# Preparing the first two pairs of a clustered attention: cluster choice on PSUM operands for pair 0, through GpSimd for pair 1, and another order of squares, halves and copies

## The chip, the cores and the metric

The kernel runs on one core of a Trainium2 chip. The metric is the device time of one execution in microseconds; lower is better. The core's engines are named as the profile names them: PE (TensorE matmuls) and PEld (its weight loads), DVE (VectorE), ACT (ScalarE), POOL (GpSimd) and SP (SyncE, whose queue issues all DMAs of this kernel). Each engine executes its own instructions in the order in which they are written for it and meets the others only at semaphores.

## The reference

Attention over clusters, for 2 batches of 8 heads, 768 positions, head width 64 and 16 centroids per head, and then two two-layer networks (512 to 2048 to 512) over its 1536 rows:

```python
q_n = q / (np.linalg.norm(q, axis=-1, keepdims=True) + 1e-06)      # k_n, c_n alike
q_assign = np.argmax(np.einsum('bhsd,hcd->bhsc', q_n, c_n), axis=-1)
k_assign = np.argmax(np.einsum('bhsd,hcd->bhsc', k_n, c_n), axis=-1)
mask = q_assign[:, :, :, None] == k_assign[:, :, None, :]
scores = scale * np.matmul(q, k.transpose(0, 1, 3, 2))
scores = np.where(mask, scores, -1000000000.0)
attn = softmax(scores)                                             # rows without the maximum
x = np.matmul(attn, v)
h = x @ w_in;  x = (np.maximum(h, 0.0) + alpha * np.minimum(h, 0.0)) @ w_out
h = x @ w_in2; out = (np.maximum(h, 0.0) + np.log1p(np.exp(-np.abs(h)))) @ w_out2
```

## The kernel before, in words

**Pairs and units.** Heads go in pairs: 8 pairs, numbered 0 to 7. A pair has 12 units: 2 heads by 6 blocks of 128 queries. Unit u computes the scores of 128 queries against 768 keys (lines 571 and 572), their row maxima (`nm`, line 577, on DVE), the exponentials (`e`, line 586, on ACT), transposes of these on PE (`pt`, line 599), their high half on ACT (`ph`, line 615) and the remainder on DVE (`pl`, line 619), and the product with the values (`o`, line 629). The stages of a unit are spread over the turns of one loop: in turn u PE does the scores of unit u, the transposes of unit u-2 and the product of unit u-4; DVE does the maximum of unit u and the remainders of unit u-2. After some 240 us the two networks follow, which the change leaves alone. All products of 32-bit numbers are made from a high half and a low half of each operand (`hi` and `lo`).

**Preparation of a pair.** Before its units a pair n needs:

- `sq0`, `sq1`: squares of its q and k by token (tile `sq` from `tok`), in two halves, on ACT for pairs 0 and 1 and on POOL for later ones; the second half also issues the load of the next pair's `tok`.
- Sums of the squares: for pair 0 by `red0` and `red1` on DVE, for later pairs by `fold0` to `fold2` on POOL, six additions of halves in place (line 341).
- `inv`: one over the norm, in three steps by `inv_norm` (lines 127 to 136): a logarithm and an exponential on ACT; a reciprocal on DVE and a product and a sum on the engine `eng` (lines 132 and 133); a scaling (line 135) and a reciprocal on DVE.
- `hik`, `lok`, `hiq`, `lq0`, `lq1`: high and low halves of k and q by dimension (from `dim`); `op0`, `op1`: six DMAs for each head that copy them into the operands `ak`, `aq`, `mk`, `mq` (line 521).
- `dk`, `dq` (or `dh`, `dl`), `de`, `dt`: dot products with the centroids (`dps`), and their transposition by token (`dt`, in PSUM).
- The cluster choice by token: `dn` scales the dots by the norms (line 428), `mx` finds the largest of 16 (line 440), `eq` compares with it and multiplies by a rank (lines 448 and 449), `m2` finds the largest rank (line 459), subtracts it (line 462) and clips at -1 (line 463). The result `oh` is 0 at the chosen cluster and -1 elsewhere.
- `ot0`, `ot1`: `oh` transposed on PE; `mr`, `rq`, `rk`: mask rows made of it by one multiplication and one addition with `mscale` and `mbias`, into `mrow` or straight into `mq` and `mk`. `va`: the halves of v, a cast on DVE and a subtraction on POOL, which then issues the load of the next pair's v.

**What sets the order.** The preparation of pair 0 and the beginning of pair 1 are written out in the list `PRELUDE`; "warm n" puts n idle transposes on PE. Everything else has a due turn in the tables `FIRST` (pair 0), `SECOND` (pair 1), `THIRD` (pair 2) and `STEADY`: an entry x of pair n is placed in turn 12(n-2) + x, rounded up, at the end of the turn if x is a whole number and ahead of its transposes otherwise. PE, ACT and DVE keep the order in which the code is written; for POOL and SP a scheduler puts the instructions in order. So what DVE does in turn 0 to 4 of pair 0 is mixed with the preparation of pair 1, whose entries lie at 12 to 16.

Of the kernel before, what the change touches and what calls it, by code (L numbers as in the profile page):

```python
# [9 lines left out]
F32 = mybir.dt.float32  # L10
# [3 lines left out]
AF = mybir.ActivationFunctionType  # L14
ALU = mybir.AluOpType
# [9 lines left out]
    hik=-1, lok=3, sq0=0, hiq=2, sq1=2, fold0=3, fold1=4, fold2=6, lq0=5, dk0=4, dq0=6, de0=6.5,  # L25
    inv0=7, lq1=8, inv1=9, dk1=9, dq1=10, inv2=10, de1=10.5, dt=11, dn=11, op0=11, mx=11.5, eq=15,
    m2=16, va=18, ot0=19, mr0=19, op1=19, ot1=20.5, mr1=20.5, mk0=20.5, mk1=20.5, go=22,
)
FIRST = dict(
    mr0=23.5, mr1=23.5, mk1=23.5,  # L30
)
SECOND = dict(
    dl0=12, dl1=12, inv0=12, de0=12.5, de1=12.5, inv1=13, inv2=13, dt=13, dn=14, mx=14, op0=14,
    eq=15, m2=16, va=18, ot0=19, mr0=19, op1=19, ot1=20.5, mr1=20.5, mk0=20.5, mk1=20.5, go=22,
)
THIRD = dict(
    hik=3, lok=3, sq0=0, hiq=4, sq1=2, fold0=4, fold1=5, fold2=6, lq0=5, dk0=5, dq0=6, de0=6.5,
    inv0=7, lq1=8, inv1=9, dk1=9, dq1=10, inv2=10, de1=10.5, dt=11, dn=11, op0=11, mx=11.5, eq=15,
    m2=16, va=18, ot0=19, mr0=19, op1=19, ot1=20.5, mr1=20.5, mk0=20.5, mk1=20.5, go=22,
)  # L40
PRELUDE = [
# [6 lines left out]
]  # L48

FINISH = [7, 9, 10, 12, 12, 14, 16]  # L50
# [3 lines left out]
P = 128  # L54
BIG = float(2.0**100)
# [3 lines left out]
def kernel(  # L59
# [20 lines left out]
    nc = tc.nc  # L80
    B, NPAIR, _, _, S = qk_dim.shape
    H = 2 * NPAIR
    C = P // H
    D = P // 2
# [10 lines left out]
    HC = 2 * C  # L95
    SCALE = float(D) ** -0.5

    const = ctx.enter_context(tc.tile_pool(name="const", bufs=1))
# [15 lines left out]
    mscale = const.tile([2 * HC, 1], F32, name="mscale")  # L114
    nc.gpsimd.memset(mscale, 1.0)
    nc.gpsimd.memset(mscale[HC : 2 * HC], BIG)
    mbias = const.tile([2 * HC, 1], F32, name="mbias")
    nc.gpsimd.memset(mbias, 1.0)
    nc.gpsimd.memset(mbias[HC : 2 * HC], 0.0)
    alpha_sb = const.tile([P, NF], F32, name="alpha_sb")  # L120
    nalpha = const.tile([P, NF], F32, name="nalpha")

    def inv_norm(out_, ss, pool, tag, eng):

        n = ss.shape[1]
        s0 = pool.tile([P, n], F32, tag=tag + "a", name="s0")
        nc.scalar.activation(out=s0, in_=ss, func=AF.Ln, bias=tiny)
        nc.scalar.activation(out=s0, in_=s0, func=AF.Exp, scale=0.5)
        yield
        s1 = pool.tile([P, n], F32, tag=tag + "b", name="s1")  # L130
        nc.vector.reciprocal(out=s1, in_=s0)
        eng.tensor_tensor(out=s1, in0=ss, in1=s1, op=ALU.mult)
        eng.tensor_tensor(out=s1, in0=s1, in1=s0, op=ALU.add)
        yield
        nc.vector.tensor_scalar(out=s1, in0=s1, scalar1=0.5, scalar2=1e-6, op0=ALU.mult, op1=ALU.add)
        nc.vector.reciprocal(out=out_, in_=s1)
        yield
# [53 lines left out]
    with ExitStack() as actx:  # L191
        ap3 = actx.enter_context(tc.tile_pool(name="ap3", bufs=3))
        first_ctx = ExitStack()
        ap1 = first_ctx.enter_context(tc.tile_pool(name="ap1", bufs=1, side="right"))
        ap2 = actx.enter_context(tc.tile_pool(name="ap2", bufs=2))
        ap4 = actx.enter_context(tc.tile_pool(name="ap4", bufs=1))
        ps_s = actx.enter_context(tc.tile_pool(name="ps_s", bufs=2, space=PSUM))
# [13 lines left out]
        ops = {}  # L211
# [80 lines left out]
        n_ = J * 4  # L292
        every = [P, n_, C]
# [3 lines left out]
        def steps_of(n):  # L297
# [49 lines left out]
            def inv():  # L347
                if "gen" not in q:
                    ss = q["ss"] if first_ else q["sq"][:, :, 0:1].rearrange("p n o -> p (n o)")
                    q["gen"] = inv_norm(q["rinv"], ss, ap1, "n", nc.vector if early else nc.gpsimd)  # L350
                next(q["gen"])

            for k in range(3):
# [70 lines left out]

            @step("dn")
            def _():
                q["dn"] = ap1.tile(every, F32, tag="dn", name="dn")
                nc.vector.tensor_tensor(
                    out=q["dn"],
                    in0=q["dt"][:, 0 : n_ * C].rearrange("p (n c) -> p n c", c=C),  # L430
                    in1=q["rinv"][:, :, None].to_broadcast(every),
                    op=ALU.mult,
                )


            @step("mx")
            def _():
                dn = q["dn"]
                q["mx"] = ap1.tile([P, n_], F32, tag="mx", name="mx")
                nc.vector.tensor_reduce(out=q["mx"], in_=dn, axis=AX.X, op=ALU.max)  # L440
                if not early:
                    nc.gpsimd.tensor_tensor(out=dn, in0=dn, in1=q["mx"][:, :, None].to_broadcast(every), op=ALU.subtract)

            @step("eq")
            def _():
                dn, r_ = q["dn"], rank[:, None, :].to_broadcast(every)
                if early:
                    nc.vector.tensor_tensor(out=dn, in0=dn, in1=q["mx"][:, :, None].to_broadcast(every), op=ALU.is_equal)  # L448
                    nc.vector.tensor_tensor(out=dn, in0=dn, in1=r_, op=ALU.mult)
                else:  # L450
                    nc.vector.scalar_tensor_tensor(
                        out=dn, in0=dn, scalar=0.0, in1=r_, op0=ALU.is_equal, op1=ALU.mult
                    )

            @step("m2")
            def _():
                dn = q["dn"]
                m2 = ap1.tile([P, n_], F32, tag="m2", name="m2")
                nc.vector.tensor_reduce(out=m2, in_=dn, axis=AX.X, op=ALU.max)
                q["oh"] = ap1.tile([P, J, 4 * C], F32R, tag="oh", name="oh")  # L460
                eng = nc.vector if first_ else nc.gpsimd
                eng.tensor_tensor(out=dn, in0=dn, in1=m2[:, :, None].to_broadcast(every), op=ALU.subtract)
                eng.tensor_scalar(
                    out=q["oh"], in0=dn.rearrange("p (j n) c -> p j (n c)", j=J), scalar1=-1.0, scalar2=None, op0=ALU.max
                )

            def onehot(t):
# [4 lines left out]
                for j in range(3):  # L472
                    nc.tensor.transpose(q["ot", t][0 : 2 * HC, j * P : (j + 1) * P], q["oh"][:, 3 * t + j, :], identr)

            def rows(t, eng):
                if t == 0:
                    q["mrow"] = ap1.tile([2 * HC, 2, HS], F32R, tag="mrow", name="mrow")
                src = q["ot", t].bitcast(F32)[0 : 2 * HC, 0:HS]
                if eng is nc.scalar:
                    nc.scalar.activation(out=q["mrow"][:, t, :], in_=src, func=AF.Identity, scale=mscale, bias=mbias)  # L480
                else:
                    nc.vector.tensor_scalar(
                        out=q["mrow"][:, t, :], in0=src, scalar1=mscale, scalar2=mbias, op0=ALU.mult, op1=ALU.add
                    )

            def straight(t, s_):

                _, _, mq, mk = res[0]
                src = q["ot", t].bitcast(F32)[:, 0:HS]
                if s_ == 0:  # L490
                    nc.scalar.activation(
                        out=mq[D : D + C, halves[t]], in_=src[0:C], func=AF.Identity, scale=mscale[0:C], bias=mbias[0:C]
                    )
                else:
                    nc.vector.tensor_scalar(
                        out=mk[D : D + C, halves[t]], in0=src[HC : HC + C], scalar1=mscale[HC : HC + C],
                        scalar2=mbias[HC : HC + C], op0=ALU.mult, op1=ALU.add,
                    )

            for t in range(2):  # L500
# [47 lines left out]
            @step("go")  # L548
            def _():
                for hh in range(2):  # L550
                    ops[n, hh] = (*res[hh], q["vv"])

            return st_

# [67 lines left out]

        def attend(key, part):
            n, hh, g = key
            vv = ops[n, hh][4]
            if part == 0:
                acc[key] = ps_o.tile([P, 512], F32, tag="o", name="o")
            for j in range(J):
                nc.tensor.matmul(  # L629
                    acc[key][:, 0:QG],  # L630
                    lhsT=vv[:, j, 2 * hh : 2 * hh + 2, :].rearrange("p a d -> p (a d)"),
                    rhs=grp[key][part][:, j, :],
                    start=part == 0 and j == 0,
                    stop=part == 1 and j == J - 1,
                )
# [386 lines left out]
```

## Time and profile before

| | us |
|---|---|
| Time, median of 3 runs (lowest, highest) | 824.72 (823.08, 827.33) |
| Time of the profiled execution | 823.56 |
| Its span, first to last instruction | 821.8 |
| PE busy | 793.8 |
| DVE busy | 603.1 |
| ACT busy | 490.7 |
| POOL busy | 345.1 |

The time is that of the whole execution, the span that of its instructions; 1.76 us of the profiled execution lie around the span. The page has the busy time of each engine, the span in 40 slices, and the chain of work that ended last, followed back from the end. What the change touches lies in the first 45 us, so the timeline of single engines in that stretch says more than the sums.

### The profile page before, as it was taken

The page shows a single profiled execution, that of the slowest core. Times are in us where ns is not written, and L with a number is a line of the kernel's source. Part 1 is how long each engine was busy: PE and PEld are TensorE (multiplying, and loading weights), DVE is VectorE, ACT ScalarE, POOL GpSimd, SP SyncE. Part 2 cuts the span into 40 slices and gives each one's busy share as a digit, 9 for nine tenths or more (in the row PEclk, how much of TensorE's full clock was granted, in tenths as well). Part 3 has the DMA queues.
Part 4 walks back from the last instruction along what each step waited for, and adds up shares of the span by engine and source line. Part 5 has one row for each costly group of instructions (what it writes and reads, how often), then busy time and mean ns, then how long its engine had stood idle before and what let it go on. Part 6 is the DMA issues. An engine that isn't in the chain of part 4 may idle for free.

```text
span 821.8 us, 11917 instructions
## 1 busy us (share of the span) xinstructions
PE 793.8 (97%) x4124; PEld 667.6 (81%) x4124; DVE 603.1 (73%) x957; ACT 490.7 (60%) x992; POOL 345.1 (42%) x350
## 2 busy tenths in 40 slices
PE   6799999999998879999999999999999999999997
PEld 5699998999997758888888888888888888888885
DVE  7899999999999977348547636977468469655443
ACT  4689998999898687247346435664355245243221
POOL 6566866775434664027025214574153045023000
PEclk9699999999999989999999999999999999999999
DMA  9876685665532254012202301411023013000102
GB/s 274 228 175 161 164 204 133 156 158 117 115 100 84 78 179 134 21 51 78 77 26 77 103 1 51 154 52 51 1 76 130 1 52 102 1 1 1 51 27 76
DMA packets 27195, 76.50 MB, mean 93 GB/s; under 512 B 4512, under 2 KB 7456, under 8 KB 27136
## 3 DMA queue, kind: packets, MB, share of 16 engines
q1 hardware_dynamic: 27136, 75.75, 32.2%
q8 instruction: 32, 0.52, 0.3%
q14 instruction: 27, 0.22, 0.1%
HBM read 49.36 MB, written 3.15 MB: 64 GB/s over the span
## 4 chain that ended last, share of the span: by engine, by line
PE 87%; DVE 7%; ACT 2%; DMA 1%; issue 1%; POOL 1%; DVEq 0%; SPq 0%; ACTq 0%; POOLq 0%
PE acc L887 33%; PE hp L828 31%; PE o L629 7%; PE pt L599 7%; PE s L572 4%; PE s L571 4%; PE dps L393 2%; DVE pl L619 1%; DVE nm L577 1%; DVE r L169 1%; DMA mk<-mrow 1%; POOL t L174 1%; DMA tok<-in_qk_tok_dram 1%; DVE m L167 0%; DVE dn L448 0%
## 5 line engine op out<-in xcount | busy, mean ns | idle before, releaser
L828 PE MATMUL hp<-xh,ih 128*128 128x512 f32 x384 | 152.3, 398 | 2.2 <-DVE gl L869 2.2
L828 PE MATMUL hp<-xl,ih 128*128 128x512 f32 x384 | 152.4, 397 | 0.0
L828 PE MATMUL hp<-xh,il 128*128 128x512 f32 x384 | 152.2, 397 | 0.0
L177 POOL TENSOR_TENSOR il<-t,ih 128x512 fp32r<-128x512 f32 x32 | 44.0, 1375 | 206.7 <-ACT ih L176 197.8
L869 DVE TENSOR_TENSOR gl<-hp,gh 128x512 fp32r<-128x512 f32 x96 | 65.9, 687 | 75.8 <-ACT gh L868 75.7
L868 ACT CAST gh<-hp 128x512 fp32r<-128x512 f32 x96 | 56.3, 586 | 93.3 <-PE acc L887 81.8
L619 DVE TENSOR_TENSOR pl<-pt,ph 128x384 fp32r<-128x384 f32 x192 | 97.4, 547 | 1.7 <-ACT ph L615 1.1
L174 POOL TENSOR_TENSOR t<-m,r 128x512 uint32<-128x512 uint32 x64 | 85.3, 1333 | 29.3 <-DVE r L169 16.4
L577 DVE TENSOR_REDUCE nm<-s 128x1 f32<-128x768 f32 x96 | 91.0, 948 | 7.8 <-PE s L572 7.4
L586 ACT ACTIVATE e<-s,nm 128x768 f32<-128x768 f32 x96 | 87.9, 916 | 7.3 <-DVE nm L577 7.0
L599 PE MATMUL pt<-ident,e 128*128 128x128 f32 x576 | 83.6, 279 | 5.8 <-DVE pl L619 5.7
L828 PEld LDWEIGHTS hp<-xh,ih 128*128 128x128 f32 x384 | 72.3, 188 | 20.1 <-DVE gl L869 2.7
L615 ACT CAST ph<-pt 128x384 fp32r<-128x384 f32 x192 | 83.5, 490 | 8.4 <-PE pt L599 7.4
L850 ACT ACTIVATE sp<-a 128x512 f32<-128x512 f32 x48 | 30.4, 633 | 96.2 <-DVE a L846 96.2
L828 PEld LDWEIGHTS hp<-xh,il 128*128 128x128 f32 x384 | 72.4, 189 | 17.6
L828 PEld LDWEIGHTS hp<-xl,ih 128*128 128x128 f32 x384 | 72.4, 189 | 17.2
L599 PEld LDWEIGHTS pt<-ident,e 128*128 128x128 f32 x576 | 67.7, 142 | 15.3 <-DVE pl L619 11.0
L887 PE MATMUL acc<-gh,oh 128*128 128x512 f32 x192 | 75.0, 402 | 4.3 <-ACT gh L868 4.3
L887 PE MATMUL acc<-gl,oh 128*128 128x512 f32 x192 | 77.0, 401 | 0.0
L887 PE MATMUL acc<-gh,ol 128*128 128x512 f32 x192 | 76.5, 399 | 0.0
L887 PE MATMUL acc<-ol,gh 128*128 128x512 f32 x192 | 75.9, 395 | 0.0
L887 PE MATMUL acc<-oh,gh 128*128 128x512 f32 x192 | 75.7, 395 | 0.0
(168 smaller groups left out, 1671.3 us busy)
## 6 DMA issues: line engine op xcount, KB each, us to landing
raw<-in_w_in_dram SPq DMA_DIRECT2D x32, 512.0 KB, 3.3
raw<-in_w_out_dram SPq DMA_DIRECT2D x32, 512.0 KB, 3.3
tok<-in_qk_tok_dram SPq DMA_DIRECT2D x8, 768.0 KB, 5.2
ak<-hi SPq DMA_DIRECT2D x32, 192.0 KB, 3.2
dim<-in_qk_dim_dram SPq DMA_DIRECT2D x6, 768.0 KB, 5.9
rawv<-in_v_dram SPq DMA_DIRECT2D x8, 384.0 KB, 3.2
aq<-hi SPq DMA_DIRECT2D x16, 192.0 KB, 3.7
mq<-hi SPq DMA_DIRECT2D x16, 192.0 KB, 4.0
```

Source lines behind the costliest of these rows:

```text
L174: nc.gpsimd.tensor_tensor(out=t.bitcast(U32), in0=mu, in1=r, op=ALU.add)
L177: nc.gpsimd.tensor_tensor(out=low, in0=t, in1=high.bitcast(F32), op=ALU.subtract)
L577: nc.vector.tensor_reduce(out=nm, in_=st[u]["s"][:, :, 0:HS], axis=AX.XY, op=ALU.max, negate=True)
L586: nc.scalar.activation(out=e.rearrange("p (a j) c -> p a (j c)", a=2), in_=st[u]["s"][:, :, 0:HS], func=AF.Exp, bias=st[u]["nm"], scale=1. ...
L599: nc.tensor.transpose(pt[:, j * P : (j + 1) * P], st[u]["e"][:, 3 * a + j, :], ident)
L615: nc.scalar.copy(out=dh, in_=src)
L619: nc.vector.tensor_tensor(out=dl, in0=src, in1=dh.bitcast(F32), op=ALU.subtract)
L629: nc.tensor.matmul(acc[key][:, 0:QG], lhsT=vv[:, j, 2 * hh : 2 * hh + 2, :].rearrange("p a d -> p (a d)"), rhs=grp[key][part][:, j, :], st ...
L828: nc.tensor.matmul(hp, lhsT=a_[:, cs], rhs=b_[:, c, ts], start=n == 0, stop=n == 3 * NC_ - 1)
L868: nc.scalar.copy(out=gh, in_=hp)
L869: nc.vector.tensor_tensor(out=gl, in0=hp, in1=gh.bitcast(F32), op=ALU.subtract)
L887: nc.tensor.matmul(accs[c], lhsT=a_, rhs=b_, start=opens and n == 0, stop=closes and n == 2)
```

## The change

For pair 0: the tile `dn` of the cluster choice lies in a slot of the PSUM pool `ps_s` and not in SBUF; `m2` makes `oh` by one comparison (1 at the chosen cluster, 0 elsewhere) and not by a subtraction and a clip; a second bias `mbias0` (0 and -2^100) fits the mask rows to that. `va` moves from `PRELUDE` to the end of turn 0. In `PRELUDE` the high half of k (`hik 0`) comes ahead of the second half of the squares (`sq1 0`), `rk0` ahead of `rk1`, and the second "warm" has 18 transposes, not 5.

For pair 1: the choice takes the form of the later pairs, a subtraction on POOL behind `mx` and one instruction on DVE for `eq` (due at 15.5, not 15), and the product and the sum of `inv` go to POOL. `go` hands over the pair's dictionary and not the tile `vv`, since `vv` is made later.

```diff
 FIRST = dict(
-    mr0=23.5, mr1=23.5, mk1=23.5,
+    mr0=23.5, mr1=23.5, mk1=23.5, va=24,
 )
 SECOND = dict(
...
-    eq=15, m2=16, va=18, ot0=19, mr0=19, op1=19, ot1=20.5, mr1=20.5, mk0=20.5, mk1=20.5, go=22,
+    eq=15.5, m2=16, va=18, ot0=19, mr0=19, op1=19, ot1=20.5, mr1=20.5, mk0=20.5, mk1=20.5, go=22,
...
-    "warm 5", "sq0 0", "centroids_high", "red0 0", "centroids_low", "sq1 0", "red1 0", "hik 0",
+    "warm 18", "sq0 0", "centroids_high", "red0 0", "centroids_low", "hik 0", "sq1 0", "lok 0",
...
+    mbias0 = const.tile([2 * HC, 1], F32, name="mbias0")
+    nc.gpsimd.memset(mbias0, 0.0)
+    nc.gpsimd.memset(mbias0[HC : 2 * HC], -BIG)
...
-                    q["gen"] = inv_norm(q["rinv"], ss, ap1, "n", nc.vector if early else nc.gpsimd)
+                    q["gen"] = inv_norm(q["rinv"], ss, ap1, "n", nc.vector if first_ else nc.gpsimd)
...
             @step("dn")
             def _():
-                q["dn"] = ap1.tile(every, F32, tag="dn", name="dn")
+                if first_:
+                    s_ = ps_s.tile([P, 2, 512], F32, tag="s", name="dn")
+                    q["dn"] = s_[:, 0, 0 : n_ * C].rearrange("p (n c) -> p n c", c=C)
+                else:
+                    q["dn"] = ap1.tile(every, F32, tag="dn", name="dn")
...
-                if not early:
+                if not first_:
                     nc.gpsimd.tensor_tensor(out=dn, in0=dn, in1=q["mx"][:, :, None].to_broadcast(every), op=ALU.subtract)
 
             @step("eq")
             def _():
                 dn, r_ = q["dn"], rank[:, None, :].to_broadcast(every)
-                if early:
+                if first_:
...
-                eng = nc.vector if first_ else nc.gpsimd
-                eng.tensor_tensor(out=dn, in0=dn, in1=m2[:, :, None].to_broadcast(every), op=ALU.subtract)
-                eng.tensor_scalar(
+                if first_:
+                    nc.vector.tensor_tensor(
+                        out=q["oh"].rearrange("p j (n c) -> p (j n) c", c=C), in0=dn,
+                        in1=m2[:, :, None].to_broadcast(every), op=ALU.is_equal,
+                    )
+                    return
+                nc.gpsimd.tensor_tensor(out=dn, in0=dn, in1=m2[:, :, None].to_broadcast(every), op=ALU.subtract)
+                nc.gpsimd.tensor_scalar(
...
+            bias = mbias0 if first_ else mbias
...
-                    ops[n, hh] = (*res[hh], q["vv"])
+                    ops[n, hh] = (*res[hh], q)
```

DVE in turns 1 to 4, before: behind the maxima of units 0 and 1 comes the whole middle part of pair 1's `inv` (tile `s_378`, `rinv`), ahead of the maximum of unit 2.

```order
L577 TENSOR_REDUCE nm<-s 128x1 x2
L131 RECIPROCAL s_378<-s_359 128x24
L132 TENSOR_TENSOR s_378<-sq,s_378 128x24
L133 TENSOR_TENSOR s_378<-s_378,s_359 128x24
L135 TENSOR_SCALAR s_378<-s_378 128x24
L136 RECIPROCAL rinv<-s_378 128x24
L577 TENSOR_REDUCE nm<-s 128x1
L619 TENSOR_TENSOR pl<-pt,ph 128x3x128 x2
```

So DVE makes product and sum (lines 132 and 133) itself. The same place of DVE now (line numbers are larger by 4 to 15):

```order
L592 TENSOR_REDUCE nm<-s 128x1
L556 CAST vv<-rawv 128x6x64 x2
L592 TENSOR_REDUCE nm<-s 128x1
L135 RECIPROCAL s_393<-s_374 128x24
L139 TENSOR_SCALAR s_393<-s_393 128x24
L140 RECIPROCAL rinv<-s_393 128x24
L592 TENSOR_REDUCE nm<-s 128x1
L634 TENSOR_TENSOR pl<-pt,ph 128x3x128 x2
```

The casts of v stand between the first two maxima, and between the reciprocal and the scaling of `s_393` DVE now waits for two instructions of POOL.

POOL at that place, before: the subtractions for `vv` stand ahead of pair 1's folds, and behind the folds come the squares of pair 2 (`sq<-tok`).

```order
L542 TENSOR_TENSOR vv<-rawv,vv 128x6x64 x2
L367 TENSOR_TENSOR lo<-dim,hi 128x768
L341 TENSOR_TENSOR sq<-sq 128x24x32
L341 TENSOR_TENSOR sq<-sq 128x24x16
L341 TENSOR_TENSOR sq<-sq 128x24x8
L341 TENSOR_TENSOR sq<-sq 128x24x4
L341 TENSOR_TENSOR sq<-sq 128x24x2
L341 TENSOR_TENSOR sq<-sq 128x24
L322 TENSOR_TENSOR sq<-tok 128x768 x2
L341 TENSOR_TENSOR sq<-sq 128x24x32
```

There is nothing for pair 1's `inv` on POOL. POOL now, from the end of pair 1's folds:

```order
L345 TENSOR_TENSOR sq<-sq 128x24
L557 TENSOR_TENSOR vv<-rawv,vv 128x6x64 x2
L136 TENSOR_TENSOR s_393<-sq,s_393 128x24
L326 TENSOR_TENSOR sq<-tok 128x768
L137 TENSOR_TENSOR s_393<-s_393,s_374 128x24
L326 TENSOR_TENSOR sq<-tok 128x768
L345 TENSOR_TENSOR sq<-sq 128x24x32
L345 TENSOR_TENSOR sq<-sq 128x24x16
L450 TENSOR_TENSOR dn<-dn,mx 128x384
L345 TENSOR_TENSOR sq<-sq 128x24x8
L371 TENSOR_TENSOR lo<-dim,hi 128x768
```

The subtractions for `vv` have moved behind the folds, and the two instructions on `s_393` that DVE waits for stand on either side of the first half of pair 2's squares.

SP's queue, before, from the load of pair 1's `tok` through the copies of pair 0's operands to the load of v for pair 1:

```order
L234 DMA tok<-in_qk_tok_dram 128x1536
L521 DMA ak<-hi 64x768 x2
L521 DMA aq<-hi 64x768
L521 DMA mq<-hi 64x768
L521 DMA mk<-lo 64x768
L521 DMA aq<-lo 64x768
L521 DMA ak<-hi 64x768 x2
L521 DMA mk<-lo 64x768
L239 DMA rawv<-in_v_dram 128x768
```

Pair 1's `tok` stands first here. SP's queue now, from the first of these copies to the load of pair 2's `tok`, which before stands three DMAs behind `rawv`:

```order
L536 DMA ak<-hi 64x768 x2
L238 DMA tok<-in_qk_tok_dram 128x1536
L536 DMA aq<-hi 64x768
L536 DMA mk<-lo 64x768
L536 DMA mq<-hi 64x768
L536 DMA aq<-lo 64x768
L536 DMA ak<-hi 64x768 x2
L536 DMA mk<-lo 64x768
L536 DMA aq<-hi 64x768
L536 DMA mq<-hi 64x768
L536 DMA aq<-lo 64x768
L238 DMA tok<-in_qk_tok_dram 128x1536
```

Pair 1's `tok` comes behind the copies of `ak`, and the load of v for pair 1 (`rawv`) no longer stands ahead of pair 2's `tok`; it now stands 13 DMAs later in the queue, behind pair 1's operands and pair 0's mask rows.

## Rows read from the trace of the kernel before

**Rows 1.** Page, part 1: busy us (share of the span) and instructions of each engine.

```profile
PE 793.8 (97%) x4124; PEld 667.6 (81%) x4124; DVE 603.1 (73%) x957; ACT 490.7 (60%) x992; POOL 345.1 (42%) x350
```

**Rows 2.** Chain in order of time, 0 to 80 us: start, us, what.

```profile
39.19 1.54 PE pt L599 x6
40.73 0.82 PE o L629 x6
```

**Rows 3.** Timeline of DVE: start, us, line, operation, out<-in, count [idle before].

```profile
14.92 2.01 DVE L448 TENSOR_TENSOR dn<-dn,mx 128x384 f32<-128x384 f32 x1
16.96 2.04 DVE L449 TENSOR_TENSOR dn<-dn,rank 128x384 f32<-128x384 f32 x1
...
20.29 0.63 DVE L463 TENSOR_SCALAR oh<-dn 128x384 fp32r<-128x384 f32 x1
...
28.89 1.38 DVE L135 TENSOR_SCALAR s<-s 128x24 f32<-128x24 f32 x1
...
30.52 0.90 DVE L577 TENSOR_REDUCE nm<-s 128x1 f32<-128x768 f32 x1
...
35.10 1.40 DVE L448 TENSOR_TENSOR dn<-dn,mx 128x384 f32<-128x384 f32 x1
36.53 1.26 DVE L449 TENSOR_TENSOR dn<-dn,rank 128x384 f32<-128x384 f32 x1
37.72 0.94 DVE L577 TENSOR_REDUCE nm<-s 128x1 f32<-128x768 f32 x1
38.59 1.01 DVE L619 TENSOR_TENSOR pl<-pt,ph 128x384 fp32r<-128x384 f32 x2
```

**Rows 4.** Timeline of POOL, the same columns.

```profile
16.47 5.55 POOL L341 TENSOR_TENSOR sq<-sq 128x768 f32<-128x768 f32 x6
28.77 2.89 POOL L322 TENSOR_TENSOR sq<-tok 128x768 f32<-128x768 f32 x2 [6.74 <-DVE s L132]
31.74 1.83 POOL L341 TENSOR_TENSOR sq<-sq 128x768 f32<-128x768 f32 x1
34.27 1.82 POOL L367 TENSOR_TENSOR lo<-dim,hi 128x768 fp32r<-128x768 f32 x1 [0.70 <-DMA aq<-lo]
```

**Rows 5.** Groups by form, 0 to 60 us: busy, mean ns of one.

```profile
L619 DVE TENSOR_TENSOR pl<-pt,ph 128x384 fp32r<-128x384 f32 x22 | 11.1, 546 | 0.0
L376 DVE SCALAR_TENSOR_TENSOR lo<-dim,hi 128x384 fp32r<-128x384 f32 x6 | 4.8, 807 | 0.4 <-ACT hi L373 0.4
...
L542 POOL TENSOR_TENSOR vv<-rawv,vv 128x384 fp32r<-128x384 f32 x4 | 4.0, 1016 | 1.4 <-DVE vv L541 1.4
L133 POOL TENSOR_TENSOR s<-s,s 128x24 f32<-128x24 f32 x1 | 0.2, 236 | 0.1
```

**Rows 6.** SP's queue: v for pair 1, `tok` for pair 2, pair 0's last mask rows.

```profile
16.53 0.77 SPq L239 DMA_DIRECT2D rawv<-in_v_dram  x1
...
19.67 0.67 SPq L234 DMA_DIRECT2D tok<-in_qk_tok_dram  x1
...
25.42 0.53 SPq L528 DMA_DIRECT2D mk<-mrow  x1
```

**Rows 7.** Tile `tok`, issue at 19.67: us from issue to landing.

```profile
DMA to landing us min/median/max: 7.8/7.8/7.8
```

**Rows 8.** PE by half microseconds: stretch, PE busy (count), granted clock, DMA share, GB/s.

```profile
26.00:26.50 0.50, 0.50 (x3) 0.50 0.99 406
...
34.00:34.50 0.50, 0.00 (x0) 0.51 0.84 313
...
40.50:41.00 0.50, 0.50 (x5) 0.67 0.92 209
```

**Rows 9.** Timeline of PE: pair 0's first dot product; the transposes of unit 1.

```profile
8.57 0.36 PE L393 MATMUL dps<-hi,chz 128*64 128x384 f32 x1 [1.77 <-ACT hi L362]
...
31.93 1.01 PE L599 MATMUL pt<-ident,e 128*128 128x128 f32 x6 [1.70 <-DVE pl L619]
```

**Rows 10.** Timeline of ACT: the squares of pair 1.

```profile
14.49 1.57 ACT L320 ACTIVATE sq<-tok 128x768 f32<-128x768 f32 x2
```

More of the change, by code (lines that the diff above doesn't have):

```diff
@@ L479, in rows @@
                 if eng is nc.scalar:
-                    nc.scalar.activation(out=q["mrow"][:, t, :], in_=src, func=AF.Identity, scale=mscale, bias=mbias)
+                    nc.scalar.activation(out=q["mrow"][:, t, :], in_=src, func=AF.Identity, scale=mscale, bias=bias)
                 else:
                     nc.vector.tensor_scalar(
-                        out=q["mrow"][:, t, :], in0=src, scalar1=mscale, scalar2=mbias, op0=ALU.mult, op1=ALU.add
+                        out=q["mrow"][:, t, :], in0=src, scalar1=mscale, scalar2=bias, op0=ALU.mult, op1=ALU.add
                     )
@@ L491, in straight @@
                     nc.scalar.activation(
-                        out=mq[D : D + C, halves[t]], in_=src[0:C], func=AF.Identity, scale=mscale[0:C], bias=mbias[0:C]
+                        out=mq[D : D + C, halves[t]], in_=src[0:C], func=AF.Identity, scale=mscale[0:C], bias=bias[0:C]
                     )
@@ L496, in straight @@
                         out=mk[D : D + C, halves[t]], in0=src[HC : HC + C], scalar1=mscale[HC : HC + C],
-                        scalar2=mbias[HC : HC + C], op0=ALU.mult, op1=ALU.add,
+                        scalar2=bias[HC : HC + C], op0=ALU.mult, op1=ALU.add,
                     )
@@ L624, in attend @@
             n, hh, g = key
-            vv = ops[n, hh][4]
+            vv = ops[n, hh][4]["vv"]
             if part == 0:
```

10 rows, old and new, of the table PRELUDE are left out of this document.

## The prediction

> **What bounds the kernel now.** I read the page first: PE is busy for 97% of the span, DVE for 73% [rows 1]. The change adds only 13 idle transposes to PE, so it can gain only where PE waits, and what is gained in the preparation lasts only if it still stands when PE becomes the bound. The chain in order of time says where that is: up to the first product over the values of unit 1, which ends at 41.55 (40.73 + 0.82), DVE steps keep coming up in it, and it ends in transposes that waited for DVE and that product [rows 2]; behind that it is PE alone. So the reading is of the first 41.6 us, engine by engine.
>
> DVE's timeline shows two costly places. In pair 0's choice two element-by-element instructions take 2.01 and 2.04 us, and the chosen clusters are ready at 20.92 (20.29 + 0.63). In pair 1's, the like take 1.40 and 1.26, and ahead of them a scaling of 24 numbers takes 1.38; the maximum of unit 2 comes behind that one, at 30.52, and the remainders of unit 2 at 38.59 [rows 3]. POOL is at work beside all of them: the folds from 16.47 and the high halves before them, the squares of pair 2 from 28.77, folds and halves from 31.74 [rows 4]. The same sort of work with one operand in PSUM, the remainders `pl`, takes 546 ns on average, and with both in SBUF (`lo`) 807 ns [rows 5].
>
> **Pair 0: the part up to the scores.** Two instructions on PSUM operands, at 0.55 as `pl`, in place of 2.01 and 2.04: 4.05 - 1.1 = 2.95 us less. One comparison in place of two instructions, of which the second took 0.63 [rows 3]: 0.6 less. The casts of v, ahead of `dn` before, lay in an idle time of DVE. The earlier high half of k is worth up to 0.8 (one of two squares of 1.57 [rows 10]). The 13 more transposes take PE at most 3.3 us (1.54 for six at the lower clock [rows 2]), of which 1.77 lie in its idle time ahead of the dots [rows 9]: a loss of up to 1.5; if they keep the clock up, the twelve dots could save half of 0.36 each, 2.2. I take 0 for that, and 0 for `rk0` ahead of `rk1` (the same instructions in another order) and for two memsets on an idle POOL. So the chosen clusters come about 3.6 us sooner (2 to 6), near 17 instead of 20.92; the scores behind them also need pair 0's operand copies, which have the same full DMA queue as before.
>
> **Where that goes.** Now the order decides. Behind the maximum of unit 1 DVE has a reciprocal and then the scaling, and the scaling now waits for two small POOL instructions, the product and the sum. Behind it in DVE's queue stand the maximum of unit 2, both remainders of unit 0 and all that follows; ACT's exponential of unit 2 waits for that maximum, PE's transposes of unit 1 for the remainders. And between product and sum POOL has the first half of pair 2's squares, which needs pair 2's `tok`.
>
> When is that there? Before, it was issued at 19.67 and landed 7.8 later, at 27.47 [rows 6, 7]. All DMA engines are busy (a share of 0.99), and 393 KB of v for pair 1 no longer go ahead of it; at 406 GB/s [rows 8] that is 1.0 us. I take 26.4; the bounds are 25.9 (1.5, as small rows move more slowly) and 27.5 (no gain).
>
> Is POOL there by then? Pair 1's folds took 5.55 beside DVE [rows 4]; they start when the squares end, 16.06 before [rows 10], now between 15.5 and 17.0, since pair 1's `tok` stands behind two copies. They end by 22.6; the subtractions for `vv` (two of 1.02 [rows 5], moved here from idle time) by 24.7; the product by 25.2 at the latest, with DVE's casts of v taking little ahead of it. POOL therefore waits for `tok`, and **what pair 0 gained upstream is lost there**, whatever its exact size.
>
> From 26.4: half the squares 1.45, the sum 0.24 [rows 4, 5], and POOL goes straight on with the other half. The scaling now meets the situation of 28.89: there it lasted 1.38, until the first of POOL's two squares was over at 30.2 [rows 3, 4], though it scales 24 numbers a lane, a thirtieth of the 768 that the maximum behind it reads in 0.90. So it is held again for 1.45. Then 0.25 to the maximum, as from 30.27 to 30.52. Sum: 26.4 + 1.45 + 0.2 + 1.45 + 0.25 = 29.75 against 30.52: **0.8 us sooner**, bounds 1.3 and -0.3.
>
> The Trainium skill ("SBUF — State Buffer", section "Who interferes with whom") states that the second SBUF port pair of VectorE is shared with GpSimd as an exclusive lock, that whoever issues first holds it for the whole instruction, and that a VectorE instruction with at most one SBUF input outside the two-port modes does not contend. The trace agrees: 1.38 us for 24 numbers, and 546 ns for `pl`. It speaks for the PSUM operands of pair 0, and against the place of the sum for pair 1; without it the scaling would be short, which is the third rival below.
>
> **Pair 1's choice.** Before, 1.40 + 1.26 = 2.66 stood ahead of the maximum of unit 4, at 37.72 [rows 3]. Now POOL makes the difference (384 numbers, under 1.2 between its folds: squares end at 29.4, a fold of 1.83 and one of about 1.2 lead to 32.5, the difference is done by 33.5), and DVE does one instruction behind that maximum, near 35.2 (29.75 + 4.58, the time from 30.52 to 35.10, + 0.9). It has both operands in SBUF, with POOL's `lo` of 1.82 alongside, so 0.6 to 1.4; I take 1.1, between the mean of `lo` and the blocked 1.40. Gain 1.5, bounds 1.2 and 2.0. The remainders of unit 2 then come at 38.59 - 0.8 - 1.5 = 36.3.
>
> **PE's clock.** Here PE stood still until 31.93, for 1.7 ahead of it [rows 9]; the granted clock fell to the lower of its two levels at 34.0 and came back between 40.5 and 41.0 [rows 8], so that the last transposes took 1.54 and the product 0.82 at least [rows 2]. PE's gap now ends at 31.1 and begins earlier, as the work ahead of it does: it is longer, so I expect the same fall. If the clock is back by 37, as the denser work behind the gap allows, transposes and product follow in about 1.4 in place of 2.36 and the gain is 3.3; if it is low until then, PE's own work is what is late and about 2.1 are left. I take the middle, 2.7.
>
> **The moved DMAs.** Pair 0's mask rows for its second head now stand behind three copies of pair 1 (192 KB, 0.94 us each at 209 GB/s [rows 8]). Issued at 25.42 before [rows 6], they come 2.8 later, and with the 7.8 of `tok` they land by 36.1; unit 6 needs them, near 38.5: hidden, and 1 us for each 1 us beyond. The load of v for pair 1 is wanted first in turn 6 as well, and its halves of pair 0 by the first product, near 35.
>
> **The rivals.** The reference is the profiled execution, 823.56, and the median of the runs, 824.72; I take the middle, 824.1.
>
> - *The forecast:* DVE waits for POOL's sum and then for the squares behind it; 2.7 less, **821.4**. Chance 0.58, own range 819.5 to 823.
> - *`tok` is no limit:* if it lands before 24.5, POOL is ready at once and the maximum of unit 2 comes near 27.7. Then 2.8 + 1.5 + 0.6 = 4.9 less, 819.2. Against it: the full DMA queue. Chance 0.13.
> - *The scaling slips in ahead of POOL's second half:* the 1.2 of the hold are saved, 3.9 less, 820.2. Against it: POOL's queue has no wait there. Chance 0.12.
> - *PSUM operands are no faster:* then unit 1's maximum is ready only 0.6 sooner than at about 28.1, pair 1's product at 28.0, the squares start there and unit 2's maximum comes 3.35 later, at 31.35, 0.8 late; pair 1's choice and the clock give back 2.1: 1.3 less, 822.8. For it: no row shows DVE writing to PSUM. Chance 0.12.
> - *Slower:* `tok` of pair 2 lands late. The maximum of unit 2 comes 3.35 after it, and pair 1's choice gives back 1.9 with the clock, so the point is 29.1. At 10.6 us from issue in place of 7.8, 30.3, it is 1.2 more, 825.3. Against it: less traffic ahead. Chance 0.05.
>
> **How the numbers follow.** 0.5% is about what a measurement of this kernel can tell from no change, 4.1 us here. The forecast alone lies within; of its 0.58 some 0.08 fall beyond with the scatter of the runs (4 us among three), of the second case 0.11, of the third 0.06, of the fourth 0.01: faster 0.26. Slower needs the last case at its worst and scatter, 0.05. The rest, 0.69, is within. The range reaches from 818.5, beyond the second case, to 824.5, which leaves out the slower one.
>
> **What would show it.** In the profile after: pair 0's two instructions near 0.55 us; DVE idle for 4 to 6 us ahead of the 24-number scaling, with POOL named; a first half of squares that starts when `tok` lands near 26.4; the scaling itself at 1.4 us; the maximum of unit 2 near 29.75; one instruction for `eq`, near 1.1. I am wrong if that idle time is short, if POOL starts these squares well before 26, or if PE still waits for DVE behind 40 us.

## The result

The changed kernel takes 816.98 us (median of 6 runs, 812.96 to 822.07) against 825.88 for the kernel before beside it: a ratio of 0.9895, 95% interval 0.9858 to 0.9931. The forecast was 821.4 with a range of 818.5 to 824.5; the time lies below it. It is faster, but not for any reason that the prediction gave: the preparation that the change rewrites comes out slower, and the gain lies in the two networks, whose code the change doesn't touch.

The profiled execution of the changed kernel took 819.76 us. Its page, part 1, answers to [rows 1]:

```profile
PE 784.9 (96%) x4137; PEld 672.7 (82%) x4137; DVE 599.4 (73%) x953; ACT 490.6 (60%) x992; POOL 345.0 (42%) x355
```

PE has 13 instructions more, as written, and 8.9 us less busy time. The first network matmul starts at 263.34 before and at 273.90 after, so in this pair of profiles the attention part lost 10.6 us; all of the gain and more lies behind it.

**The networks.** PE's timeline, kernel before, at 400 us (start, us, line, out<-in):

```profile
400.13 0.40 PE L887 MATMUL acc<-gh,oh 128*128 128x512 f32 x1
400.37 0.40 PE L887 MATMUL acc<-gl,oh 128*128 128x512 f32 x1
400.60 0.40 PE L887 MATMUL acc<-gh,ol 128*128 128x512 f32 x1
400.83 0.40 PE L887 MATMUL acc<-gh,oh 128*128 128x512 f32 x1
```

The same of the changed kernel:

```profile
400.24 0.39 PE L843 MATMUL hp<-xl,ih 128*128 128x512 f32 x1
400.46 0.39 PE L843 MATMUL hp<-xh,il 128*128 128x512 f32 x1
400.69 0.39 PE L843 MATMUL hp<-xh,ih 128*128 128x512 f32 x1
400.92 0.39 PE L843 MATMUL hp<-xl,ih 128*128 128x512 f32 x1
```

A matmul starts every 0.233 us before and every 0.227 after, in both layers of the networks. By stretches, 280 to 800 us (length; busy us and count of PE, PEld, DVE, ACT, POOL; granted clock, DMA share, GB/s), before:

```profile
280.00:800.00 520.00, 513.39 (x2184) 412.27 (x2184) 331.74 (x485) 248.41 (x443) 176.61 (x131) 0.99 0.18 59
```

and after:

```profile
280.00:800.00 520.00, 512.94 (x2250) 423.16 (x2249) 342.78 (x502) 255.62 (x457) 182.13 (x135) 0.99 0.19 63
```

The same clock, 0.99, the same busy time of PE, and 66 matmuls more in the same 520 us. It is neither the clock nor a wait: each matmul takes less. The networks have 2304 of them; at 6 to 7 ns each that is 14 to 16 us. From the start of the first one to the start of the last four (one row of the timeline) it is 552.2 us before and 537.7 after.

**The preparation.** DVE of the changed kernel, which answers to [rows 3]:

```profile
14.04 0.57 DVE L456 TENSOR_TENSOR dn<-dn,mx 128x384 f32<-128x384 f32 x1
14.64 0.57 DVE L457 TENSOR_TENSOR dn<-dn,rank 128x384 f32<-128x384 f32 x1
...
15.83 0.56 DVE L470 TENSOR_TENSOR oh<-dn,m 128x384 fp32r<-128x384 f32 x1
...
20.47 1.26 DVE L510 TENSOR_SCALAR mk<-ot,mscale,mbias 16x384 fp32r<-16x384 f32 x2 [3.61 <-ACT mq L506]
...
23.44 0.96 DVE L592 TENSOR_REDUCE nm<-s 128x1 f32<-128x768 f32 x1 [0.35 <-PE s L587]
...
31.50 1.42 DVE L139 TENSOR_SCALAR s<-s 128x24 f32<-128x24 f32 x1 [4.33 <-POOL s L137]
...
33.18 0.89 DVE L592 TENSOR_REDUCE nm<-s 128x1 f32<-128x768 f32 x1
...
37.76 0.95 DVE L592 TENSOR_REDUCE nm<-s 128x1 f32<-128x768 f32 x1
38.62 1.10 DVE L459 SCALAR_TENSOR_TENSOR dn<-dn,rank 128x384 f32<-128x384 f32 x1
39.64 1.01 DVE L634 TENSOR_TENSOR pl<-pt,ph 128x384 fp32r<-128x384 f32 x2
```

Pair 0's clusters are chosen at 16.39, not 20.92. Then DVE waits 4.33 us for POOL's sum, the scaling takes 1.42, and unit 2's maximum comes at 33.18, 2.7 later than before; pair 1's choice gives 1.6 of it back, and the remainders of unit 2 are 1.05 late. POOL, which answers to [rows 4]:

```profile
27.32 0.24 POOL L136 TENSOR_TENSOR s<-sq,s 128x24 f32<-128x24 f32 x1 [0.53 <-DVE s L135]
29.80 1.47 POOL L326 TENSOR_TENSOR sq<-tok 128x768 f32<-128x768 f32 x1 [2.25 <-DMA tok<-in_qk_tok_dram]
31.23 0.23 POOL L137 TENSOR_TENSOR s<-s,s 128x24 f32<-128x24 f32 x1
31.42 1.47 POOL L326 TENSOR_TENSOR sq<-tok 128x768 f32<-128x768 f32 x1
```

Product, wait for pair 2's `tok`, half of the squares, the sum: it is the chain that was forecast, but 3.4 us later. Two more views say why. ACT, which answers to [rows 10]:

```profile
18.17 1.57 ACT L324 ACTIVATE sq<-tok 128x768 f32<-128x768 f32 x2 [4.33 <-DMA tok<-in_qk_tok_dram]
19.77 0.66 ACT L506 ACTIVATE mq<-ot,mbias,mscale 16x384 fp32r<-16x384 f32 x1
```

and SP's queue, which answers to [rows 6]:

```profile
7.90 1.17 SPq L536 DMA_DIRECT2D ak<-hi  x2
9.17 0.53 SPq L238 DMA_DIRECT2D tok<-in_qk_tok_dram  x1
...
12.02 0.82 SPq L536 DMA_DIRECT2D aq<-lo  x1
...
20.91 0.33 SPq L238 DMA_DIRECT2D tok<-in_qk_tok_dram  x1
```

Pair 1's `tok`, issued behind two copies into `ak`, lands 9.0 us later; before it was issued first, at 7.73, and landed after 6.1. ACT stands still for it, and pair 0's mask rows (`mq`, line 506) stand behind these squares in ACT's queue; DVE's own (`mk`, line 510) wait 3.61 us for those and end at 21.73. Pair 0's operand copies also stand behind that `tok`: `aq<-lo`, the last one that the first scores read, is issued at 12.02 and lands 9.6 us later (5.9 before), at 21.6, where before it landed at 18.9. PE's first scores start right behind it (the profile puts the wait down to `mk<-lo`, another of these copies):

```profile
21.79 0.66 PE L586 MATMUL s<-ak,aq 128*128 128x384 f32 x1 [4.73 <-DMA mk<-lo]
22.24 0.52 PE L587 MATMUL s<-mk,mq 80*128 80x384 f32 x1
```

In the kernel before, the product with the mask rows was the one that waited, and it waited for DVE:

```profile
21.69 0.63 PE L571 MATMUL s<-ak,aq 128*128 128x384 f32 x1
23.24 0.69 PE L572 MATMUL s<-mk,mq 80*128 80x384 f32 x1 [0.93 <-DVE mk L495]
```

and unit 0's maximum on DVE came behind it:

```profile
24.61 0.96 DVE L577 TENSOR_REDUCE nm<-s 128x1 f32<-128x768 f32 x1 [0.83 <-PE s L572]
```

So of the 4.5 us by which the clusters are chosen sooner, 1.2 reach unit 0's maximum (23.44, at 24.61 before): the scores waited for the choice before, and for the copies now. Pair 2's `tok` is issued at 20.91, 1.2 later than before, and lands 8.7 after that, at 29.6.

### The profile page after: what moved, and what is told of

The parts are those of the page before. It is cut to its first block, busy times and chain, and to the rows that moved or that the text cites. A ratio compares the mean times of both kernels' runs of the same rounds, so it can differ in the third digit from the quotient of the medians.

```text
span 817.8 us, 11947 instructions
## 1 busy us (share of the span) xinstructions
PE 784.9 (96%) x4137; PEld 672.7 (82%) x4137; DVE 599.4 (73%) x953; ACT 490.6 (60%) x992; POOL 345.0 (42%) x355
## 4 chain that ended last, share of the span: by engine, by line
PE 76%; DVE 11%; DMA 5%; POOL 3%; issue 2%; ACT 2%; SPq 0%; DVEq 0%; POOLq 0%; ACTq 0%
PE acc L902 29%; PE hp L843 27%; PE pt L614 6%; PE o L644 6%; PE s L587 3%; PE s L586 3%; DVE r L173 2%; DVE pl L634 2%; DMA tok<-in_qk_tok_dram 2%; DVE nm L592 1%; DMA mq<-hi 1%; POOL t L178 1%; DVE m L168 1%; DMA mq<-mrow 1%; PE dps L397 1%
## 5 line engine op out<-in xcount | busy, mean ns | idle before, releaser
L843 PE MATMUL hp<-xh,ih 128*128 128x512 f32 x384 | 149.8, 391 | 2.7 <-DVE gl L884 2.4
L843 PE MATMUL hp<-xl,ih 128*128 128x512 f32 x384 | 150.0, 391 | 0.0
L843 PE MATMUL hp<-xh,il 128*128 128x512 f32 x384 | 149.7, 390 | 0.0
L614 PE MATMUL pt<-ident,e 128*128 128x128 f32 x576 | 85.4, 282 | 6.8 <-DVE pl L634 6.8
L614 PEld LDWEIGHTS pt<-ident,e 128*128 128x128 f32 x576 | 68.9, 145 | 17.2 <-DVE pl L634 12.6
L586 PE MATMUL s<-ak,aq 128*128 128x384 f32 x192 | 70.6, 367 | 4.7 <-DMA mk<-lo 4.7
```

What stands on the lines that cost most here:

```text
L586: nc.tensor.matmul(s[:, c, 0:HS], lhsT=aq[:, qs], rhs=ak[:, ks], start=True, stop=False)
L614: nc.tensor.transpose(pt[:, j * P : (j + 1) * P], st[u]["e"][:, 3 * a + j, :], ident)
L843: nc.tensor.matmul(hp, lhsT=a_[:, cs], rhs=b_[:, c, ts], start=n == 0, stop=n == 3 * NC_ - 1)
```

## The experiments

The first theory: the new constant `mbias0` does it. The kernel places its tiles on the left side of SBUF one behind another, and the weights of the networks on the right side. The new tile takes 32 bytes of each partition, so all that comes behind it moves by 32: the high halves of the tokens (`xh`) from byte 17856 to 17888, their low halves and `gh` and `gl` likewise; the weights `ih` stay at 188384. Taken modulo 64, the tokens go from 0 to 32, and the weights stand at 32 in both. The rival: the other preparation, or the chip, is what made the networks faster.

**A tile of 32 bytes alone.** The kernel before and:

```diff
+    pad0 = const.tile([2 * HC, 1], F32, name="pad0")
+    nc.gpsimd.memset(pad0, 0.0)
```

> The kernel before with one unused 32-byte constant tile, nothing else: every tile on the left side of SBUF moves by 32 bytes, as the change's new constant moves it; weights stay. Address theory: the 512-column matmuls of the networks start every 0.227 us and not every 0.233, some 15 us less in all, about 810 us. Rival (the gain came from the change of the preparation, or from the chip): 0.233, about 825 us.

Measured: 815.99 us (10 runs, 810.88 to 822.96), ratio 0.9871 (0.9832 to 0.9909). The networks, in the same columns as above:

```profile
280.00:800.00 520.00, 512.96 (x2249) 423.26 (x2248) 339.81 (x497) 253.82 (x452) 180.03 (x134) 0.99 0.19 62
```

2249 matmuls, as after the change. A tile that nobody uses makes this kernel as fast as the change does. The total is not the 810 expected: 14 us less in the networks, 10 in all.

**The change without its shift.** The changed kernel with both constants in one tile:

```diff
-    mbias = const.tile([2 * HC, 1], F32, name="mbias")
+    both_ = const.tile([2 * HC, 2], F32, name="mbias")
+    mbias, mbias0 = both_[:, 0:1], both_[:, 1:2]
...
-    mbias0 = const.tile([2 * HC, 1], F32, name="mbias0")
```

> The changed kernel with its new constant stored as a second column of the old constant's tile, so that all other tiles lie where they lay before. Address theory: the networks' matmuls go back to 0.233 us, 15 us more, 828 to 834 us, slower than before, because attention alone lost time. Rival: as the changed kernel, about 817 us, with 0.227.

Measured: 829.72 us (10 runs, 826.74 to 837.68), ratio to the kernel before 1.0059 (1.0024 to 1.0093).

```profile
280.00:800.00 520.00, 513.22 (x2197) 412.48 (x2196) 334.37 (x488) 252.31 (x449) 180.69 (x134) 0.99 0.18 60
```

The gain is gone, and what is left is what the change of the preparation does with tokens and weights where they were: 2 to 8 us more. Beside the lone tile, which has the places of the changed kernel, it can't be told apart by time (ratios 0.9895 and 0.9871).

**Which places.** Three more kernels, each one run: two pads of 32 bytes on the left; one pad of 32 bytes on the right side, in front of the weights; and a pad on either side.

```diff
+            wpad = ctx.enter_context(tc.tile_pool(name="wpad", bufs=1, side="right"))
+            nc.gpsimd.memset(wpad.tile([P, 8], F32, name="wpad"), 0.0)
```

> The kernel before with two unused 32-byte constant tiles: left tiles move by 64 bytes, so their place within 64 bytes is that of before. If the place within 64 bytes decides: 0.233 us a matmul, about 825 us. If any shift will do, or a coarser grid counts: 0.227, about 810 us.

> The kernel before with a 32-byte pad on the right side of SBUF: the weights move by 32 bytes, tokens (the moving operand) stay where they are. If only equal places of weights and tokens within 64 bytes count: 0.227 us a matmul, about 810 us. If the tokens' own place counts: 0.233, about 825 us.

> The kernel before with both the left tiles and the weights moved by 32 bytes: tokens at 32 within 64 bytes, weights at 0, the fourth pairing after 0 and 32 (before), 32 and 32, 0 and 0. If equal places count: 0.233 us a matmul and 39.8 at 400 us as before, about 826 us. If only tokens at 0 with weights at 32 are slow: 0.227, about 813 us.

Measured: 830.69, 815.15 and 828.64 us. The networks with the pad on the right:

```profile
280.00:800.00 520.00, 511.98 (x2249) 422.51 (x2249) 339.62 (x497) 253.95 (x452) 179.97 (x134) 0.99 0.19 62
```

and with a pad on either side:

```profile
280.00:800.00 520.00, 512.53 (x2197) 411.32 (x2196) 334.34 (x489) 252.59 (x450) 180.66 (x134) 1.00 0.18 60
```

All kernels of this study, by the places modulo 64 and by the time from the start of the first network matmul to the start of the last four:

| tokens, weights | kernels | us |
|---|---|---|
| 0, 32 | before; two pads; the two with both constants in one tile | 552.2; 552.5; 550.4, 551.8 |
| 32, 0 | a pad on either side | 550.9 |
| 32, 32 | after (twice); one pad on the left; five variants below | 537.7, 536.1; 538.3; 536.1 to 537.8 |
| 0, 0 | one pad on the right | 538.4 |

The four pairings settle it: what counts is whether the moving and the stationary operand stand at equal places, not where either stands. Unequal costs 14 us here. Averaged over the networks, a matmul starts every 226.7 or 226.8 ns in the nine profiles with equal places and every 233.2 or 233.3 in the five with unequal ones. It makes no difference that in the second half of the last network the tokens are the stationary operand and the weights the moving one. The attention's products over the values (256 columns) show nothing of the kind: at the upper clock they start every 134.8 to 136.0 ns, whether the places of `ph` and `vv` are equal or not. Only shifts of 32 and 64 bytes were tried, and all tiles of a side were moved at once; which part of the chip it is that the two operands meet in was not measured.

**The preparation.** Now the second theory: its loss has two causes, the order (pair 1's `tok` behind the copies) and the split of pair 1's norm between DVE and POOL. The rival: the DMA queue is late anyway, or something else stands right behind. All these kernels have the places of the changed one, but for one that is marked.

The changed kernel with `tok` first:

```diff
-    "warm 18", "sq0 0", "centroids_high", "red0 0", "centroids_low", "hik 0", "sq1 0", "lok 0",
-    "red1 0", "hiq 0", "lq0 0", "dk0 0", "dq0 0", "inv0 0", "lq1 0", "inv1 0", "de0 0", "dk1 0",
+    "warm 18", "sq0 0", "centroids_high", "red0 0", "centroids_low", "sq1 0", "red1 0", "hik 0",
+    "lok 0", "hiq 0", "lq0 0", "dk0 0", "dq0 0", "inv0 0", "lq1 0", "inv1 0", "de0 0", "dk1 0",
```

> The changed kernel, in which the first pair's second half of squares stands ahead of its copy to high halves again, as before, so that pair 1's tok is issued ahead of the copies into ak. Theory (tok lands late because it queues with the copies, and DVE's scaling then waits for POOL): tok of pair 1 lands 6 us after its issue and not 9, near 14; unit 2's maximum comes at 30.5 or sooner, not at 33.2; the first networks matmul about 3 us sooner; 812 to 814 us. Rival (the landing depends on the load of the queues, not on the order): 817 us, maximum near 33.

Measured: 813.12 us (809.27 to 816.47), ratio 0.9859 (0.9813 to 0.9905). Pair 1's `tok` landed 7.1 us after its issue and ACT waited 1.06 us for it. POOL and DVE in this kernel:

```profile
28.57 1.47 POOL L326 TENSOR_TENSOR sq<-tok 128x768 f32<-128x768 f32 x1 [3.50 <-DMA tok<-in_qk_tok_dram]
```

```profile
30.26 1.42 DVE L139 TENSOR_SCALAR s<-s 128x24 f32<-128x24 f32 x1 [5.58 <-POOL s L137]
31.94 0.90 DVE L592 TENSOR_REDUCE nm<-s 128x1 f32<-128x768 f32 x1
```

Half right: pair 1 was on time, PE's first scores started at 19.77 and unit 0's maximum at 20.95, but pair 2's `tok`, issued at 18.97, took 9.4, so that the maximum of unit 2 came at 31.94 and not by 30.5. Of the 2.5 us gained by unit 0, half went into a longer wait for POOL, 5.58 us.

The changed kernel with pair 1's norm on DVE:

```diff
-                    q["gen"] = inv_norm(q["rinv"], ss, ap1, "n", nc.vector if first_ else nc.gpsimd)
+                    q["gen"] = inv_norm(q["rinv"], ss, ap1, "n", nc.vector if early else nc.gpsimd)
```

> The changed kernel with pair 1's product and sum of the norm on DVE again, the rest as changed. Theory (DVE waits for POOL, which does half of pair 2's squares between them): the wait of 4.3 us ahead of the scaling goes, the scaling is 0.2 to 1.4 us, unit 2's maximum comes near 29, some 4 us sooner; 813 to 814 us. Rival (something else is late right behind, as the scores or the copies): maximum moves, total 816 to 818.

Measured: 814.95 us (812.71 to 817.48), ratio 0.9891 (0.9843 to 0.9939). DVE:

```profile
27.06 0.18 DVE L137 TENSOR_TENSOR s<-s,s 128x24 f32<-128x24 f32 x1
27.28 0.18 DVE L139 TENSOR_SCALAR s<-s 128x24 f32<-128x24 f32 x1
...
29.13 0.96 DVE L592 TENSOR_REDUCE nm<-s 128x1 f32<-128x768 f32 x1 [1.33 <-PE s L587]
```

and POOL:

```profile
29.26 2.89 POOL L326 TENSOR_TENSOR sq<-tok 128x768 f32<-128x768 f32 x2 [2.91 <-DMA tok<-in_qk_tok_dram]
```

The wait is gone, and the maximum comes 4.05 us sooner, with the scores late right behind it. The same scaling takes 0.18 us while POOL stands idle, and 1.42 beside POOL's square, until that one ends (31.42 + 1.47 = 32.89). The times of these two kernels alone can't be told from that of the changed one.

Both edits together:

> Both edits: tok first and pair 1's norm on DVE, so that only the PSUM choice, the one comparison, the POOL subtraction and the new order of values remain. If the two causes are separate and add: about 810 us; if they are one chain: as the better of the two, 812 to 814.

Measured: 809.59 us (808.13 to 812.54), ratio 0.9823 (0.9784 to 0.9861). All four runs lie below the ten of the changed kernel from two sets (812.96 to 822.07), if by little: a version that beats both kernels. DVE:

```profile
25.55 0.96 DVE L592 TENSOR_REDUCE nm<-s 128x1 f32<-128x768 f32 x1 [1.68 <-PE s L587]
...
33.20 0.94 DVE L459 SCALAR_TENSOR_TENSOR dn<-dn,rank 128x384 f32<-128x384 f32 x1 [1.58 <-POOL dn L450]
```

The maximum of unit 2 comes 7.6 us sooner than in the changed kernel. Alone the edits gave 1.2 and 4.05: the two causes stand in one row, and either alone left the other to wait for. The same with both constants in one tile, so with the places of before:

> The kernel with tok first and pair 1's norm on DVE (809.59 us), its new constant as a second column of the old tile, so that all addresses are those of before. If addresses and preparation add: 13 to 14 us more, 822 to 824, which is what the preparation alone gives back against the kernel before (825.6). If the preparation's gain needs the faster networks: as before.

Measured: 822.90 us (10 runs), ratio 0.9937 (0.9912 to 0.9962). So the mended preparation alone is worth 3 to 7 us, and the places add to it. Which of its parts earn this, with the 18 idle transposes and the later `va` still among them, was not separated.

From the other side, the kernel before with the first pair's choice in PSUM alone, and then with pair 1's choice as well:

```diff
-                q["dn"] = ap1.tile(every, F32, tag="dn", name="dn")
+                if first_:
+                    s_ = ps_s.tile([P, 2, 512], F32, tag="s", name="dn")
+                    q["dn"] = s_[:, 0, 0 : n_ * C].rearrange("p (n c) -> p n c", c=C)
...
+                if first_:
+                    nc.vector.tensor_tensor(
+                        out=q["oh"].rearrange("p j (n c) -> p (j n) c", c=C), in0=dn,
+                        in1=m2[:, :, None].to_broadcast(every), op=ALU.is_equal,
+                    )
+                    return
```

> The kernel before with the first pair's choice in PSUM and one comparison for two alone; its new constant moves the left tiles by 32 bytes. Against the kernel before with only the 32-byte tile (816 us): if the choice is on the path, 3 to 4 us less, 812 to 813; if it is hidden behind the copies into mk, no difference, 816.

> The kernel before with the first pair's choice in PSUM and one comparison, and pair 1's choice with its subtraction on POOL, but with the order, the warm-up count and the values' place of before. If the POOL subtraction is worth the 2 us that DVE's two instructions are longer in the PSUM-alone run: 809 to 811 us; if it is hidden or paid back by a wait for POOL: 812.

Measured: 811.97 us (809.15 to 820.37), ratio 0.9864 (0.9798 to 0.9929), and 813.97 (808.94 to 819.63), ratio 0.9833 (0.9774 to 0.9892). With such a scatter in four runs each, neither is told from the other, nor from the lone tile's 815.99. The traces say more. DVE and POOL of the first:

```profile
15.61 0.57 DVE L456 TENSOR_TENSOR dn<-dn,mx 128x384 f32<-128x384 f32 x1
...
26.78 0.96 DVE L592 TENSOR_REDUCE nm<-s 128x1 f32<-128x768 f32 x1 [0.65 <-PE s L587]
...
31.43 1.13 DVE L456 TENSOR_TENSOR dn<-dn,mx 128x384 f32<-128x384 f32 x1
32.59 2.05 DVE L457 TENSOR_TENSOR dn<-dn,rank 128x384 f32<-128x384 f32 x1
```

```profile
14.61 1.81 POOL L371 TENSOR_TENSOR lo<-dim,hi 128x768 fp32r<-128x768 f32 x1
```

The same instruction takes 0.57 us with `dn` in PSUM, while POOL is at work until 16.42, and 1.13 in pair 1 with `dn` in SBUF, with POOL at work there too. Unit 2's maximum comes at 26.78; in the five profiles with the preparation of before it comes at 27.97 to 30.52. Pair 1's two take 3.18 us; the second kernel replaces them by a wait and one instruction, 1.56 + 1.36:

```profile
35.35 1.36 DVE L459 SCALAR_TENSOR_TENSOR dn<-dn,rank 128x384 f32<-128x384 f32 x1 [1.56 <-POOL dn L450]
```

The instruction that was saved is paid back as a wait for POOL.

The changed kernel once more, beside these:

> The changed kernel once more beside these, for the share of the preparation: 816 to 818 us, 3 us more than either mended kernel; its tok landing 9 us after its issue, and DVE's wait of 4 us ahead of the scaling, as before.

Measured: 817.40 us (814.29 to 820.59), ratio 0.9885 (0.9839 to 0.9932); pair 1's `tok` landed after 9.3 us, DVE waited 5.39 us for POOL, and unit 2's maximum came at 33.11.

## Why the prediction was wrong

- **The step that failed** is half a sentence: "0 ... for two memsets on an idle POOL". The tile that they fill moves every tile behind it, and that was worth 14 us in the networks: the whole gain, and more. The reading took for granted that code which the change leaves alone keeps its time.
- **Pair 0's choice: right.** 0.57 us each for 0.55 forecast, the clusters 4.5 sooner for 3.6 (2 to 6). The choice itself is 3.6 shorter (3.55 us from `dn` on, 7.18 before); the other 0.9 goes with the clock, for which the prediction took 0. From 10.1 to 13.5 us PE's granted clock was at the lower of its two levels before, and it wasn't after. In the seven profiles where it stayed up until then `dn` starts at 12.6 to 12.8, in the other seven at 13.5 to 14.4. One of the seven has only 5 in the second "warm", and one that fell has 18, so the longer warm-up didn't make it sure.
- **"Squares end between 15.5 and 17.0": wrong.** They ended at 19.74, since `tok` behind two copies landed 9.0 us after its issue. The prediction let POOL's folds wait for them, and took the queue of pair 0's copies to be as before. But those came later too: `aq<-lo` landed 2.7 us later, and in eight of the nine kernels with the new choice of pair 0 the first scores start 0.13 or 0.14 us behind that landing.
- **That the gain is lost in DVE's wait for POOL: right.** DVE was idle for 4.33 us (4 to 6 forecast), with POOL named, and the scaling took 1.42 (1.4 forecast). That POOL waited for `tok` was in part luck: its product, forecast for 25.2 at the latest, ended at 27.56, and with `tok` there at 26.4 POOL itself would have been late.
- **The landing of pair 2's `tok` at 26.4: wrong**, it was 29.6. It was issued at 20.91 and not at 19.67, as the prediction took it, and needed 8.7 us and not 7.8. Added to the landing, the 3.35 us of the slower rival give 32.95, and the maximum came at 33.18. That rival, with its turning point of 29.1 and a chance of 0.05, is what the preparation did. The other profiles show how weak a base one landing was: in all 14 it is 6.8 to 9.4 us after the issue, early or late. The base for the maximum was as weak: 30.52 is the latest of the five with the preparation of before.
- **Pair 1's choice: right** by size, 1.10 us for 1.1, and a gain of 1.6 for 1.5.
- **PE's clock: low for longer.** With PE idle for 4.73 us ahead of the first scores, the granted clock was at the lower of its two levels from 20.3 to 40.8 without a break. Before, with PE idle for 3.63 us until pair 0's clusters were chosen, it was low from 20.4 to 27.2 and again from 34.0 to 40.8 [rows 8]. So it was not back by 37: of the two cases between which the prediction took the middle, it was the one with the smaller gain.
- **What the preparation is worth in the end:** with tokens and weights where they were, 2 to 8 us lost, for 2.7 gained in the forecast. The transposes of unit 3, on PE, start at 40.2 to 41.1 in the three profiles with the preparation of the change and at 37.7 to 39.2 in the five with that of before: 2 us late. Of the 10.6 us at the start of the networks much is chance: the five profiles with the preparation of before have it at 263.3 to 270.3 (mean 268.2), the three with that of the change at 270.0 to 273.9 (mean 271.7). In between PE isn't alone, as the prediction took it to be: from 42 to 262 us its waits, for copies and for DVE, add up to 3.6 us before and 6.9 after, and to 3.6 to 9.2 over all profiles. What sets them stays open, and so does why the lone tile gave 10 us where the networks gave 14.

The Trainium skill ("SBUF — State Buffer", section "Who interferes with whom") holds where the prediction used it: 0.57 us on PSUM operands beside a busy POOL, and 0.18 or 1.42 us for a scaling without and with POOL's square. The same section says that the shared port pair is the only cause of contention and that TensorE's two read ports, for the moving operand and for the weights, are independent. The runs here show an effect of the two operands' addresses that this doesn't foresee: with equal places a matmul starts every 0.227 us, with unequal ones every 0.233. Whether that is contention at the ports was not measured.

## What to carry to other kernels

A change that adds, removes or resizes one tile moves all that come behind it, so ask where the operands of the longest stage stand before and after; a pad of 32 bytes is a cheap thing to try, and when untouched code changes its time, undo the shift before explaining the edit. (The effect is shown here for streams of 512-column matmuls alone.) When half of an engine's small computation is handed to another engine, look at what stands between the pieces in that engine's queue: here a load from memory did, and it took all that had been gained ahead of it. Put the load whose consumer has a long queue behind it first: here, issued ahead of the copies, it brought the first scores 2 us forward, though these read the copies.

## What the chip showed that was not expected

- The pitch of 512-column matmuls depends on the places of their two SBUF operands: 0.227 us where tokens and weights stand at equal places modulo 64 bytes (32 and 32, or 0 and 0), 0.233 where they differ by 32, at a granted clock of 0.99 or 1.00; 14 us of 826 in this kernel.
- The load of pair 1's `tok` (768 KB) landed 5.7 to 7.1 us after its issue in nine of the ten profiles in which it went ahead of the copies into the operands, and 8.9 to 9.3 in the four in which it went behind two of them; the tenth, of the kernel with both choices changed, took 9.0 though it went first.
